# The last output column of a down projection in two halves of 256 features

## Chip, cores, metric

One core of one Trainium2 chip. The metric is the device time of one launch in microseconds (us), as the median of several runs. The profile is one execution, and its span (first to last instruction) is about 1.8 us shorter than the time of the profiled run. The record labels each run fast, slow (over 1.5% above the fastest of the same kernel, for a kernel on one core) or unknown.

## The reference, cut to what matters

```python
x = A_x                                    # [1, 2048, 512], bf16
xn = _layernorm(x, axis=-1)
return x + _A_ref(xn, A_w_r, A_w_i) + _B_ref(xn, B_w_gate, B_w_up, B_w_down)
# _A_ref: irfft2(rfft2(xn) * W), a spectral filter
# _B_ref: h = gelu(xn @ w_gate) * (xn @ w_up)   with 1792 hidden features
#         h @ w_down                            [2048, 1792] x [1792, 512]
```

## The kernel before

The kernel keeps everything in on-chip memory. A first stage loads and normalizes, a long middle stage makes the gate and up products (`h`, stored as tiles `hT`) with the spectral branch woven in, and a last stage makes the output. That last stage is what the change touches. The 2048 rows are 16 "columns" of 128 rows. For each column, 14 matmuls of the down projection and one of the inverse transform add up in one PSUM tile (the accumulator that the matmuls write) of 128x512 f32. VectorE then adds the residual `x` and SyncE's queue stores the column.

```python
    def down(c):
        sb, cl = c // 4, c % 4
        y_ps = ps.tile([P, D], F32, name="y_ps", tag="S", bufs=4)          # P = 128, D = 512
        for f in range(NFC):                                               # NFC = 14
            nc.tensor.matmul(y_ps[:], lhsT=hT[sb, f][:, cl * P:(cl + 1) * P], rhs=Wd_sb[:, f, :],
                             start=(f == 0), stop=False)
        nc.tensor.matmul(y_ps[:], lhsT=late["RI"][:, c, :], rhs=late["yt"][:, c, :], start=False, stop=True)
        y_sb = pw.tile([P, D], BF16, name="y_sb", bufs=3)
        nc.sync.dma_start(out=y_sb[:], in_=x_v[:, c, :])
        nc.vector.tensor_tensor(out=y_sb[:], in0=y_ps[:], in1=y_sb[:], op=ALU.add)
        nc.sync.dma_start(out=out_v[:, c, :], in_=y_sb[:])
    # ... (all earlier stages cut)
    for c in range(NC + 2):                                                # NC = 16
        if c < NC:
            idstep(c)        # last step of the spectral branch, writes yt
        if c >= 2:
            down(c - 2)
```

Of the kernel before, what the change touches and what calls it, by code (L numbers as in the profile page):

```python
# [10 lines left out]
P = 128  # L11
BF16 = mybir.dt.bfloat16
F32 = mybir.dt.float32
I32 = mybir.dt.int32
ALU = mybir.AluOpType
AF = mybir.ActivationFunctionType

S = 2048
D = 512
NC = 16  # L20
# [3 lines left out]
NFC = DF // P  # L24
# [99 lines left out]
def kernel(  # L124
# [11 lines left out]
    nc = tc.nc  # L136
# [6 lines left out]
    out_v = out.rearrange("b (p c) d -> p c (b d)", c=NC)  # L143
# [5 lines left out]
    ps = ctx.enter_context(tc.tile_pool(name="ps", bufs=2, space=bass.MemoryType.PSUM))  # L149
# [6 lines left out]
    Wd_sb = pc.tile([P, NFC, D], BF16, name="Wd_sb")  # L156
# [4 lines left out]
    late = {}  # L161
# [300 lines left out]
    hT = {}  # L462
# [22 lines left out]

    def down(c):
        sb, cl = c // 4, c % 4
        y_ps = ps.tile([P, D], F32, name="y_ps", tag="S", bufs=4)
        for f in range(NFC):
            nc.tensor.matmul(y_ps[:], lhsT=hT[sb, f][:, cl * P:(cl + 1) * P], rhs=Wd_sb[:, f, :],  # L490
                             start=(f == 0), stop=False)
        nc.tensor.matmul(y_ps[:], lhsT=late["RI"][:, c, :], rhs=late["yt"][:, c, :], start=False, stop=True)  # L492
        y_sb = pw.tile([P, D], BF16, name="y_sb", bufs=3)
        nc.sync.dma_start(out=y_sb[:], in_=x_v[:, c, :])
        nc.vector.tensor_tensor(out=y_sb[:], in0=y_ps[:], in1=y_sb[:], op=ALU.add)  # L495
        nc.sync.dma_start(out=out_v[:, c, :], in_=y_sb[:])


    first_columns()
# [45 lines left out]
    for c in range(NC + 2):  # L545
        if c < NC:
            idstep(c)
        if c >= 2:
            down(c - 2)
# [30 lines left out]
```

## Time and profile before

| | before |
|---|---|
| time, median of 3 runs | 185.38 us (185.33 to 185.46) |
| span of the profiled run | 183.77 us |
| TensorE busy | 172.2 us, 94% |
| last stage, first down matmul to end of span | 58.86 us |
| tail, start of the last matmul to end of span | 4.37 us |

The page's busy times (engine, busy us, share of the span, instructions) and its chain of the work that ended last:

```profile
PE 172.2 (94%) x1080; PEld 92.7 (50%) x1080; DVE 116.1 (63%) x273; ACT 97.8 (53%) x181; POOL 17.2 (9%) x52
...
PE 83%; DVE 4%; DMA 3%; POOL 3%; issue 3%; ACT 2%; ACTq 0%
```

PE is TensorE's matmuls, and they make 83% of the chain. Other engines' work is worth shortening where TensorE has nothing to do. That is so in the opening load stage (TensorE was busy for 13.6 of the first 20 us, the transfer engines for 94%), which this change leaves alone, and in the tail. This is the timeline of that tail, for TensorE and VectorE (start us, duration us, engine, line, operation, what it writes and reads, and in brackets what ended its idle time):

```profile
176.17 0.38 PE L492 MATMUL y_ps<-yt,RI_t 128*128 128x512 bf16 x1
...
176.38 3.18 PE L490 MATMUL y_ps<-Wd_sb,hT 128*128 128x512 bf16 x14
...
179.40 0.38 PE L492 MATMUL y_ps<-yt,RI_t 128*128 128x512 bf16 x1
179.82 0.69 DVE L495 TENSOR_TENSOR y_sb<-y_ps,y_sb 128x512 bf16<-128x512 f32 x1 [2.55 <-PE y_ps L492]
```

The first line is the last matmul of column 14, then come the 15 of column 15, one every 215.8 ns: (179.404 - 176.167) / 15. The sum waits for the last of them and takes 0.69 us. SyncE's view of the same tail (the issue of the last store, and what SyncE waited for after 180 us: total us, times, longest us):

```profile
180.54 0.33 SPq L496 DMA_DIRECT2D out_dram<-y_sb  x1
```

```profile
SPq L496 <- DVE y_sb L495: 2.9, 1, 2.9
SPq L575 <- DMA out_dram<-y_sb: 1.1, 1, 1.1
SPq L575 <- PEq L575: 1.1, 2, 0.9
```

So the order at the end is: last matmul, sum, store, landing of the store, closing waits (L575), end. A semaphore is a counter through which an engine learns that something is done; a store has landed when its semaphore has the full count. To see when the store moves its data, here are 40 slices of the window from 180.8 to 182.4 us, so 0.04 us each (share of the transfer engines in tenths, and rate):

```profile
DMA  0000000000000047899999973100000000000000
GB/s 0 0 0 0 0 0 0 0 0 0 0 0 0 0 154 256 307 358 410 358 384 358 333 231 103 26 0 0 0 0 0 0 0 0 0 0 0 0 0 0
```

Data flows in 12 slices, 0.48 us, of the 1.68 us from issue to landing. By the trace's packet records the first data packet starts 0.84 us after the issue, the last ends at 1.33 us, and the landing follows 0.35 us later.

### The profile page before, as it was taken

The numbers are of one execution on the slowest core, as the hardware profiler recorded it, in microseconds if no ns is written. First come the engines' busy times: TensorE is split into PE (matmuls) and PEld (weight loads), VectorE is DVE, ScalarE is ACT, GpSimd is POOL, SyncE is SP. The second block draws the span as 40 slices with busy tenths as digits, with TensorE's granted clock in tenths as the row PEclk, the third lists the DMA queues.
The fourth block names the chain that finished last, engine by engine and source line by source line (L and its number), as shares of the span: only waits on it lengthen the run. The fifth ranks groups of instructions, "written<-read, shape, count | busy, mean of one in ns | idle before, by whom it ended". The sixth has DMA issues, their size and how long they took to land.

```text
span 183.8 us, 3059 instructions
## 1 busy us (share of the span) xinstructions
PE 172.2 (94%) x1080; PEld 92.7 (50%) x1080; DVE 116.1 (63%) x273; ACT 97.8 (53%) x181; POOL 17.2 (9%) x52
## 2 busy tenths in 40 slices
PE   0699999899899999999999999999999999999991
PEld 0598974354445544554555554445445445445440
DVE  2679959972954599679778879835541541541611
ACT  2533568559888986988988875453211211211100
POOL 0000042177642000000000000000000000000000
PEclk9999999999999999999999999999999999999998
DMA  4999971404995001201392210100122221221210
GB/s 147 325 384 382 339 181 30 86 0 110 227 136 159 0 13 44 62 14 43 80 356 83 59 48 13 44 13 2 61 83 67 78 86 62 76 95 60 83 57 29
DMA packets 22062, 19.37 MB, mean 105 GB/s; under 512 B 8288, under 2 KB 20576, under 8 KB 22048
## 3 DMA queue, kind: packets, MB, share of 16 engines
q1 hardware_dynamic: 20816, 17.22, 33.2%
q0 software_dynamic: 416, 1.32, 3.1%
q10 hardware_dynamic: 816, 0.66, 1.1%
q8 instruction: 8, 0.13, 0.3%
q14 instruction: 6, 0.05, 0.1%
HBM read 13.41 MB, written 2.10 MB: 84 GB/s over the span
## 4 chain that ended last, share of the span: by engine, by line
PE 83%; DVE 4%; DMA 3%; POOL 3%; issue 3%; ACT 2%; ACTq 0%
PE y_ps L490 26%; PE g_ps L477 22%; PE u_ps L480 22%; DMA Wu_sb<-in_B_w_up_dram 3%; PE dp L346 2%; PE ep L358 2%; PE yp L445 2%; PE gp L430 2%; PE y_ps L492 2%; DVE hT L484 2%; PE bp L333 2%; ACT xn L273 1%; ACT ge L483 1%; DVE stats L257 1%; PE tp L306 1%
## 5 line engine op out<-in xcount | busy, mean ns | idle before, releaser
L477 PE MATMUL g_ps<-xnT,Wg_sb 128*128 128x512 bf16 (+2 forms) x276 | 62.3, 347 | 1.1 <-DMA xnT<-xn 0.5
L480 PE MATMUL u_ps<-xnT,Wu_sb 128*128 128x512 bf16 (+2 forms) x276 | 60.9, 344 | 0.1
L490 PE MATMUL y_ps<-Wd_sb,hT 128*128 128x512 bf16 x224 | 51.0, 379 | 0.0
L484 DVE TENSOR_TENSOR hT<-u_ps,ge 128x512 bf16<-128x512 f32 (+2 forms) x69 | 40.1, 583 | 15.0 <-PE u_ps L480 7.5
L483 ACT ACTIVATE ge<-g_ps 128x512 bf16<-128x512 f32 (+2 forms) x69 | 35.5, 520 | 21.2 <-PE g_ps L477 19.6
L480 PEld LDWEIGHTS <-Wu_sb 128*128 128x128 bf16 x276 | 26.6, 101 | 23.1 <-DMA Wu_sb<-in_B_w_up_dram 0.4
L477 PEld LDWEIGHTS <-Wg_sb 128*128 128x128 bf16 x276 | 25.8, 102 | 19.6 <-issue 2.0
L490 PEld LDWEIGHTS <-hT 128*128 128x128 bf16 x224 | 21.3, 98 | 23.1
L495 DVE TENSOR_TENSOR y_sb<-y_ps,y_sb 128x512 bf16<-128x512 f32 x16 | 11.1, 692 | 30.2 <-PE y_ps L492 30.2
L451 ACT CAST yf<-yp 128x512 bf16<-128x512 f32 x16 | 9.2, 587 | 37.3 <-PE yp L445 37.3
L361 ACT CAST E<-ep 64x512 bf16<-64x512 f32 x32 | 18.5, 579 | 3.7 <-PE ep L358 3.4
L339 ACT CAST Bs<-bp 128x512 bf16<-128x512 f32 x16 | 9.0, 586 | 3.4 <-PE bp L333 3.4
L339 ACT CAST ds<-dp 128x512 bf16<-128x512 f32 x16 | 9.2, 607 | 1.2 <-PE dp L346 1.2
L273 ACT ACTIVATE xn<-x_t,nb,rstd 128x512 bf16<-128x512 bf16 x12 | 9.4, 810 | 0.4 <-POOL nb L265 0.4
L339 ACT CAST Gs<-gp 128x512 bf16<-128x512 f32 x16 | 8.6, 591 | 1.4 <-PE gp L430 1.4
L257 DVE BATCH_NORM_STATS2 stats<-x_t 128x6 f32<-128x512 bf16 x14 | 9.2, 667 | 0.0
L383 DVE TENSOR_TENSOR X<-E 128x512 bf16<-128x512 bf16 x8 | 3.4, 426 | 8.6 <-ACT E L361 8.6
L306 PE MATMUL tp<-CT,xn 128*128 128x128 bf16 x16 | 2.0, 266 | 5.8 <-DVE xn L291 5.7
L445 PEld LDWEIGHTS <-Gs 128*128 128x128 bf16 x64 | 4.8, 98 | 3.3
L492 PE MATMUL y_ps<-yt,RI_t 128*128 128x512 bf16 x16 | 6.1, 379 | 0.0
L346 PE MATMUL dp<-CT,Bs 128*128 128x128 bf16 x64 | 6.0, 219 | 0.0
L333 PE MATMUL bp<-RF_t,xf 128*128 128x128 bf16 x64 | 5.4, 219 | 0.6 <-DVE xf L323 0.6
(67 smaller groups left out, 120.3 us busy)
## 6 DMA issues: line engine op xcount, KB each, us to landing
y_sb<-in_A_x_dram SPq DMA_DIRECT2D x16, 128.0 KB, 2.1
F<-F SPq DMA_DIRECT2D x32, 64.0 KB, 2.0
out_dram<-y_sb SPq DMA_DIRECT2D x16, 128.0 KB, 1.7
Wd_sb<-in_B_w_down_dram SPq DMA_DIRECT2D x1, 1792.0 KB, 8.8
x_t<-in_A_x_dram SPq DMA_DIRECT2D x3, 512.0 KB, 11.7
Wg_sb<-in_B_w_gate_dram SPq DMA_DIRECT2D x1, 768.0 KB, 9.0
Wu_sb<-in_B_w_up_dram SPq DMA_DIRECT2D x1, 768.0 KB, 10.6
Wg_sb<-in_B_w_gate_dram SPq DMA_DIRECT2D x2, 256.0 KB, 5.1
```

Of the source, the lines that this page charges most:

```text
L257: tc.keep_in_program_order(V.bn_stats(out=stats[:], in_=x_t[:, c, :]))
L273: nc.scalar.activation(out=xn[:, c, :], in_=x_t[:, c, :], func=AF.Identity, bias=nb[:, c:c + 1], scale=rstd[:, c:c + 1]))
L339: nc.scalar.copy(out=o, in_=i)
L346: nc.tensor.matmul(dp[:, q // 2, q % 2, :], lhsT=Bs[:, q, G].rearrange("p c r a -> p (c r a)"), rhs=FQ[q], start=(q == 0), stop=(q == 3), ...
L361: nc.scalar.copy(out=E[64 * h:64 * h + 64, r], in_=ep[64 * r:64 * r + 64])
L477: nc.tensor.matmul(gp[:], lhsT=Wg_sb[:, e, fc * P:(fc + 1) * P], rhs=rhs[:, e, :], start=(e == 0), stop=(e == NE - 1))
L480: nc.tensor.matmul(up[:], lhsT=Wu_sb[:, e, fc * P:(fc + 1) * P], rhs=rhs[:, e, :], start=(e == 0), stop=(e == NE - 1))
L483: nc.scalar.activation(out=ge[:], in_=gp[:], func=AF.Gelu_apprx_tanh)
L484: nc.vector.tensor_tensor(out=hT[sb, fc][:, o:o + w], in0=up[:], in1=ge[:], op=ALU.mult)
L490: nc.tensor.matmul(y_ps[:], lhsT=hT[sb, f][:, cl * P:(cl + 1) * P], rhs=Wd_sb[:, f, :], start=(f == 0), stop=False)
L492: nc.tensor.matmul(y_ps[:], lhsT=late["RI"][:, c, :], rhs=late["yt"][:, c, :], start=False, stop=True)
L495: nc.vector.tensor_tensor(out=y_sb[:], in0=y_ps[:], in1=y_sb[:], op=ALU.add)
```

## The change

The intent is to shorten the tail. In two halves, the first half's sum and store run under the second half's matmuls, and what is left exposed is a sum and a store of half the size.

```diff
     def down(c):
         sb, cl = c // 4, c % 4
-        y_ps = ps.tile([P, D], F32, name="y_ps", tag="S", bufs=4)
-        for f in range(NFC):
-            nc.tensor.matmul(y_ps[:], lhsT=hT[sb, f][:, cl * P:(cl + 1) * P], rhs=Wd_sb[:, f, :],
-                             start=(f == 0), stop=False)
-        nc.tensor.matmul(y_ps[:], lhsT=late["RI"][:, c, :], rhs=late["yt"][:, c, :], start=False, stop=True)
         y_sb = pw.tile([P, D], BF16, name="y_sb", bufs=3)
         nc.sync.dma_start(out=y_sb[:], in_=x_v[:, c, :])
-        nc.vector.tensor_tensor(out=y_sb[:], in0=y_ps[:], in1=y_sb[:], op=ALU.add)
-        nc.sync.dma_start(out=out_v[:, c, :], in_=y_sb[:])
+        w = D if c < NC - 1 else D // 2
+        for o in range(0, D, w):
+            y_ps = ps.tile([P, w], F32, name="y_ps", tag="S", bufs=4)
+            for f in range(NFC):
+                nc.tensor.matmul(y_ps[:], lhsT=hT[sb, f][:, cl * P:(cl + 1) * P], rhs=Wd_sb[:, f, o:o + w],
+                                 start=(f == 0), stop=False)
+            nc.tensor.matmul(y_ps[:], lhsT=late["RI"][:, c, :], rhs=late["yt"][:, c, o:o + w],
+                             start=False, stop=True)
+            nc.vector.tensor_tensor(out=y_sb[:, o:o + w], in0=y_ps[:], in1=y_sb[:, o:o + w], op=ALU.add)
+            nc.sync.dma_start(out=out_v[:, c, o:o + w], in_=y_sb[:, o:o + w])
```

## The prediction

> **What bounds the kernel now.** The page gives TensorE 94% busy of a 183.8 us span at a mean granted clock of 0.997, and the chain of work that ended last is 83% TensorE. The last stage is a pure TensorE stream: by the timeline, each output column of the down projection has 15 matmuls of 512 columns, 215.7 ns apart (3.24 us), with no idle time. Only the tail after the last matmul is exposed. The timeline of the last 8 us shows it: the first matmul of column 15 starts at 176.38, the last at 179.40; the residual sum (VectorE, 128x512) runs from 179.82 for 0.69 us; the store is issued at 180.54 and lands after about 1.7 us (median of the 16 stores); the span ends at 183.8. The DMA slices show data moving only from 181.3 to 181.85, about 0.4 us of work at 399 GB/s. So from the last matmul to the end there are about 4.2 us, of which 0.69 us (sum) and about 0.4 us (data) depend on the size of the last piece; the rest is latency and closing barriers.
>
> **What the change does.** It touches column 15 alone.
> - *Removed from the tail:* the last residual sum covers 256 instead of 512 features. The groups by form show the same kind of VectorE instruction (PSUM f32 + bf16 to bf16) at 683 ns for 128x512, 413 ns for 128x256 and 287 ns for 128x128. The Trainium skill, "VectorE: DVE Perf Modes", section on the TRN2 errata, gives (N+151)/0.96 ns, which is 691 for 512 (the trace: 691) and 424 for 256. I take 0.42: a gain of 0.27 us.
> - *Removed from the tail:* half the bytes of the last store, an estimate of 0.15 us (64 KB at about 390 GB/s is 0.17 us, against 0.33). The fixed part stays[...]. Rows become 512 bytes, so the gain may be less.
> - *Added on the critical path:* 30 matmuls of 256 columns instead of 15 of 512. The gate and up products already have 128x256 matmuls with a fresh weight load each, four in 0.437 us, 109.2 ns apart. So 3.276 us for 3.237: +0.04 us.
> - *Added off the path:* one more VectorE instruction and one more store (0.34 us of issue) under the second half's 1.6 us of matmuls. The first half's store should be issued near 178.5 and land near 180.2, before the second moves data. It uses another PSUM buffer, so no new wait.
> - *Moved:* the load of the residual is written ahead of the matmuls. It was already issued long before it is needed (172.35 for column 15), so nothing follows, unless the instruction order of other columns shifts.
>
> **Sum.** +0.04 - 0.27 - 0.15 = -0.38 us: 185.38 to 185.0 us, range 184.75 to 185.25. Faster by over 2%: 0.005; within 2%: 0.99; slower: 0.005.
>
> **What would show it.** TensorE starts column 15 at the same time; its last matmul starts near 179.55; the last VectorE sum is 0.42 us and starts near 179.86; the last store is issued near 180.3 and lands in about 1.55 us; the span shrinks to about 183.4. Right in sign but off in size: look at the store's landing and the matmul spacing.
>
> **What would make it wrong.** The second sum waiting for the first half's store to land (shared tile y_sb): then slower by about 0.4 us. Weight loads not hiding under 256-column matmuls here: up to +0.3 us. A store whose time to landing does not shrink with its bytes: gain only 0.23. A different instruction order in earlier columns: either way by a few tenths.

## The result, and the profile after

The first four runs had a median of 185.39 us (185.09 to 185.59) against 185.42 of four runs before. The ratio was 0.9984, with a 95% interval of 0.9961 to 1.0007. Ratios here are the mean time of one kernel's fast runs over that of the other's of the same rounds, so not quite the ratio of the medians. The means of all four runs against all four give 0.9997, so this first ratio is soft. Six more runs, in the experiments below, gave 185.18 us against 185.48, a ratio of 0.9978 (0.9963 to 0.9994). The second interval is wholly below 1.

The timeline of the tail after (columns as before):

```profile
176.49 0.38 PE L496 MATMUL y_ps<-yt,RI_t 128*128 128x512 bf16 x1
...
176.71 1.69 PE L494 MATMUL y_ps<-Wd_sb,hT 128*128 128x256 bf16 x14
...
178.23 0.27 PE L496 MATMUL y_ps<-yt,RI_t 128*128 128x256 bf16 x1
...
178.34 1.69 PE L494 MATMUL y_ps<-Wd_sb,hT 128*128 128x256 bf16 x14
178.54 0.42 DVE L498 TENSOR_TENSOR y_sb<-y_ps,y_sb 128x256 bf16<-128x256 f32 x1 [0.95 <-PE y_ps L496]
...
179.87 0.27 PE L496 MATMUL y_ps<-yt,RI_t 128*128 128x256 bf16 x1
180.18 0.42 DVE L498 TENSOR_TENSOR y_sb<-y_ps,y_sb 128x256 bf16<-128x256 f32 x1 [1.21 <-PE y_ps L496]
```

The first half's sum, at 178.54, lies wholly under the second half's matmuls. So does the issue of its store, as SyncE's line from 178 us on shows (two issues, the first at 179.00):

```profile
179.00 1.97 SPq L499 DMA_DIRECT2D out_dram<-y_sb  x2
```

The second sum took 0.42 us and waited for TensorE alone. SyncE's last issue and its waits after 180 us, and the rate in the same window of 180.8 to 182.4 us:

```profile
180.63 0.33 SPq L499 DMA_DIRECT2D out_dram<-y_sb  x1
```

```profile
SPq L499 <- DVE y_sb L498: 1.2, 1, 1.2
SPq L578 <- PEq L578: 1.1, 2, 0.9
SPq L578 <- DMA out_dram<-y_sb: 1.0, 1, 1.0
```

```profile
DMA  0000000000000000148999620000000000000000
GB/s 0 0 0 0 0 0 0 0 0 0 0 0 0 0 0 0 64 154 256 333 320 257 167 77 13 0 0 0 0 0 0 0 0 0 0 0 0 0 0 0
```

Half the bytes took 9 slices (0.36 us) instead of 12. The engines are as busy (9 tenths at the peak) at a lower rate: 333 GB/s against 410. The packet records say the same: a packet of 512 bytes took 26.8 ns in the mean and one of 1024 bytes 45.8. So rows of 512 bytes cost the engines more per byte here than rows of 1024.

**Absolute times mislead here.** The profiled run after came to column 15 at 176.49, 0.32 us later than the one before, though nothing that the change touches had run yet. The two traces show the same instructions in the same order on VectorE, ScalarE, GpSimd and SyncE up to column 15 (some matmul records are missing, so TensorE's can't be compared one by one). So the two spans (183.77 and 183.71) look almost equal while the tail is clearly shorter. The remedy is to anchor both traces at an event ahead of the change. From the start of column 14's last matmul, in ns, read from the trace's records:

| ns from the anchor to | before | after | difference |
|---|---|---|---|
| start of the last sum | 3654 | 3691 | +37 |
| end of the last sum | 4345 | 4114 | -231 |
| issue of the last store | 4373 | 4143 | -230 |
| landing of the last store | 6050 | 5723 | -327 |
| end of the span | 7607 | 7219 | -388 |

Term by term: +37 for the matmuls, -268 for the sum, -97 for the landing, and -61 between landing and end (the last 1 ns is at the issue). The last was in nobody's calculation, and -97 is less than the -150 predicted for the store. Both are followed up below.

### The profile page after: what moved, and what is told of

It reads as the page before. It is cut to its first block, busy times and chain, and to the rows that moved or that the text cites. A ratio compares the mean times of both kernels' runs of the same rounds, so it can differ in the third digit from the quotient of the medians.

```text
span 183.7 us, 3076 instructions
## 1 busy us (share of the span) xinstructions
PE 171.3 (93%) x1078; PEld 94.2 (51%) x1095; DVE 116.3 (63%) x274; ACT 97.9 (53%) x181; POOL 17.5 (10%) x52
## 4 chain that ended last, share of the span: by engine, by line
PE 78%; DVE 7%; ACT 5%; issue 4%; POOL 3%; DMA 2%; ACTq 0%
PE y_ps L494 26%; PE u_ps L480 21%; PE g_ps L477 19%; DVE hT L484 2%; PE y_ps L496 2%; PE yp L445 2%; PE dp L346 2%; PE ep L358 2%; PE gp L430 2%; DMA x_t<-in_A_x_dram 2%; ACT xn L273 2%; PE bp L333 1%; ACT Bs L339 1%; ACT E L361 1%; PE tp L306 1%
## 5 line engine op out<-in xcount | busy, mean ns | idle before, releaser
L477 PE MATMUL g_ps<-xnT,Wg_sb 128*128 128x512 bf16 (+2 forms) x266 | 61.3, 346 | 1.6 <-DMA xnT<-xn 0.8
L494 PE MATMUL y_ps<-Wd_sb,hT 128*128 128x512 bf16 (+1 forms) x233 | 50.7, 366 | 0.2
L494 PEld LDWEIGHTS <-hT 128*128 128x128 bf16 x238 | 22.7, 98 | 22.0
L498 DVE TENSOR_TENSOR y_sb<-y_ps,y_sb 128x512 bf16<-128x512 f32 (+1 forms) x17 | 11.2, 660 | 29.8 <-PE y_ps L496 29.8
L496 PE MATMUL y_ps<-yt,RI_t 128*128 128x512 bf16 (+1 forms) x17 | 6.2, 366 | 0.1
```

Source lines behind the costliest of these rows:

```text
L477: nc.tensor.matmul(gp[:], lhsT=Wg_sb[:, e, fc * P:(fc + 1) * P], rhs=rhs[:, e, :], start=(e == 0), stop=(e == NE - 1))
L498: nc.vector.tensor_tensor(out=y_sb[:, o:o + w], in0=y_ps[:], in1=y_sb[:, o:o + w], op=ALU.add)
```

## The experiments

The theory: the change acts on the tail alone, through four terms (matmuls, sum, landing, closing), and the gain exists because the first half hides under the second half's matmuls. The rivals: the difference is scatter of the opening load stage; it comes from the moved residual load; or small pieces are good wherever they stand.

The kernels ran with five rounds each (five or six runs), but for the first result (four runs) and the last two of the table, which had one look each. The record names another chip for each of the three groups of timed runs and for the last two, so times are compared only within a group. To compare profiles, I use the last stage's length, from the first down matmul to the end of the span. It includes every column. The control `move_only` agrees with the profile of the kernel before within 4 ns. The diffs are against the changed kernel, except where said.

| kernel | last stage, us | against before | median of time, us | ratio (95% interval) |
|---|---|---|---|---|
| before | 58.857 | | 185.38 | |
| move_only | 58.853 | -0.004 | 185.60 | 1.0004 (0.9989 to 1.0018) |
| after, first profile | 58.469 | -0.388 | 185.39 | 0.9984 (0.9961 to 1.0007) |
| after_again | 58.472 | -0.385 | 185.18 | 0.9978 (0.9963 to 0.9994) |
| matmul_halves_only | 58.902 | +0.045 | 185.62 | 1.0018 (0.9992 to 1.0045) |
| halves_one_store | 58.625 | -0.232 | 185.58 | 1.0001 (0.9985 to 1.0017) |
| sum_halves_only | 58.920 | +0.063 | 185.66 | 1.0015 (0.9994 to 1.0036) |
| split_384_128 | 58.246 | -0.611 | 184.82 | 0.9969 (0.9957 to 0.9982) |
| split_448_64 | 58.587 | -0.270 | 185.18 | 1.0004 (0.9981 to 1.0027) |
| all_columns_halves | 59.432 | +0.575 | 186.10 | 1.0048 (1.0031 to 1.0066) |
| before_four_more_loads | 58.614 | -0.243 | 185.20 | 0.9979 (0.9952 to 1.0006) |
| split_384_128_three_more_loads | 58.025 | -0.832 | 184.60 | 0.9954 (0.9923 to 0.9986) |
| before_one_more_load | 58.830 | -0.027 | 187.43, single run | |
| after_seven_more_loads | 58.476 | -0.381 | 187.10, single run | |

The kernel before had medians of 185.48, 185.37 and 185.40 us in the three groups of timed runs. In the group of the last two kernels its one run took 187.44 us; they came to the first down matmul 2 us later (126.8 us). I use only the last stage of these two, and their times not at all.

**The control first.** `move_only` keeps only the new line order of the change.

```diff
-        w = D if c < NC - 1 else D // 2
+        w = D if c < NC - 0 else D // 2    # true for every column: none is halved
```

> Only the line order of the change (the residual's load written ahead of the matmuls), no halves: the instructions of every engine stand in the same order as before. Theory: ratio 1 within 0.0005; it also shows the scatter of such a comparison. Rival (the moved load matters): a gain or loss of 0.2 us or more.

Its instructions stand in the same order as before (in the trace on VectorE, ScalarE, GpSimd and SyncE; some of TensorE's records are missing), and its last stage differs by 4 ns. Its profiled run took 186.17 us of time, though, because it came to the first down matmul at 125.51 us. Over the 12 profiles of the timed kernels that moment lies between 124.65 and 125.51 us. So the scatter of what comes ahead of it is about 0.9 us, and the last stage repeats within a few ns. The moved load does nothing. An effect of 0.2 us has to be read from the anchored trace, and the time can only confirm it roughly.

**The changed kernel again.**

> The changed kernel itself, more rounds. Theory (only the tail after the last matmul moves): from the start of column 14's last matmul to the end of the span 7.22 us against 7.61 us before, so 0.3 to 0.45 us less in time, ratio 0.9976 to 0.9984. Rival (nothing but scatter of the opening load stage, where the one profile of after stood 0.32 us later at column 15 than before): ratio within 0.0005 of 1.

The tail came out at 7.22 us a second time, and the time fell by 0.3 us by the medians. The rival of pure scatter falls, by the repeated tail above all: the interval of the ratio ends at 0.9994, just below 1.

**The matmuls alone.** Halves for TensorE, into one 512-wide tile, with one sum and one store (the diff is shortened).

```diff
+        y_ps = ps.tile([P, D], F32, name="y_ps", tag="S", bufs=4)
         for o in range(0, D, w):
-            y_ps = ps.tile([P, w], F32, ...)
             # 15 matmuls into y_ps[:, o:o + w], with skip_group_check=True (cut)
-            nc.vector.tensor_tensor(... o:o + w ...); nc.sync.dma_start(... o:o + w ...)
+        nc.vector.tensor_tensor(out=y_sb[:], in0=y_ps[:], in1=y_sb[:], op=ALU.add)
+        nc.sync.dma_start(out=out_v[:, c, :], in_=y_sb[:])
```

> The last column's 15 matmuls of 512 become 30 of 256 into one 512-wide tile, with one sum and one store as before: the cost of the change alone. Theory: +0.04 us (30 x 109.2 ns against 15 x 215.7 ns), the distance from column 14's last matmul to the sum's start 3.69 us against 3.65; ratio about 1.0002, not to be told from 1 by the time. Rival (fresh weight loads cost more here): over +0.15 us.

The timeline of TensorE in this kernel's last column:

```profile
176.02 0.38 PE L496 MATMUL y_ps<-yt,RI_t 128*128 128x512 bf16 x1
176.23 1.69 PE L494 MATMUL y_ps<-Wd_sb,hT 128*128 128x256 bf16 x14
177.76 0.27 PE L496 MATMUL y_ps<-yt,RI_t 128*128 128x256 bf16 x1
177.87 1.69 PE L494 MATMUL y_ps<-Wd_sb,hT 128*128 128x256 bf16 x14
179.40 0.27 PE L496 MATMUL y_ps<-yt,RI_t 128*128 128x256 bf16 x1
```

The second half starts 0.11 us after the first half's last matmul, with no gap: 15 matmuls in 1.638 us, 109.2 ns each, with a fresh weight load for every one. The sum starts 3.692 us after the anchor, 38 ns later than before. The cost of the change is those 38 ns; the stage grew by 45.

**Everything but the split store.**

```diff
-        w = D if c < NC - 1 else D // 2
-        for o in range(0, D, w):
+        ends = ((0, D),) if c < NC - 1 else ((0, 256), (256, 256))
+        for o, w in ends:
             # matmuls as in the changed kernel (cut)
             nc.vector.tensor_tensor(out=y_sb[:, o:o + w], in0=y_ps[:], in1=y_sb[:, o:o + w], op=ALU.add)
-            nc.sync.dma_start(out=out_v[:, c, o:o + w], in_=y_sb[:, o:o + w])
+        nc.sync.dma_start(out=out_v[:, c, :], in_=y_sb[:])
```

> Matmuls and sums in halves, one 128 KB store after the second sum: the change without its split store. Theory: the store is issued at the same 4.14 us after column 14's last matmul as in the changed kernel, but takes 1.68 us to land instead of 1.58, so the end comes 0.10 us later than there: 0.23 us less than before. Rival (the gain is all the smaller store): no gain against before.

The store went out 4.144 us after the anchor, as in the changed kernel, and took 1.674 us to land, as before. The stage gained 0.232 us. The time didn't show it (1.0001, with an interval that still holds 0.9987), which is the scatter again. The end came 0.156 us later than in the changed kernel, not the expected 0.10: the landing makes 0.094 of it, and the closing, from landing to end, was 1.557 us instead of 1.496, which I had not expected. So the closing term goes with the split store, not with the matmuls or the sum.

**Small pieces without anything to hide them.** One 512-wide accumulation, then two sums and two stores (the diff is shortened).

```diff
         # 15 matmuls of 512 columns into one y_ps, as before
+        for o in range(0, D, w):
+            nc.vector.tensor_tensor(out=y_sb[:, o:o + w], in0=y_ps[:, o:o + w], in1=y_sb[:, o:o + w], op=ALU.add)
+            nc.sync.dma_start(out=out_v[:, c, o:o + w], in_=y_sb[:, o:o + w])
```

> 15 matmuls of 512 as before, then two sums of 256 and two stores of 64 KB one after the other. Theory (the gain comes from hiding the first half's sum and store under the second half's matmuls): the second sum ends 0.75 to 0.8 us after the first starts, later than the single sum's 0.69; the last store lands 0.10 us sooner; together -0.1 to +0.05 us against before, no clear gain. Rival (smaller pieces are what counts): as fast as the changed kernel, -0.3 us.

VectorE's last column and SyncE's last issues in this kernel:

```profile
179.69 0.76 DVE L497 TENSOR_TENSOR y_sb<-y_ps,y_sb 128x256 bf16<-128x256 f32 x2 [2.55 <-PE y_ps L495]
```

```profile
180.15 0.81 SPq L498 DMA_DIRECT2D out_dram<-y_sb  x2
```

The two sums end 0.76 us after the first began, against 0.69 for the single one, and the two issues in one queue start 0.424 us apart (180.149 and 180.573). The second sum had ended at 180.451, so its store also stood behind the first one's issue. It also took 1.638 us to land, not about 1.58 as expected. So the landing came 0.120 us later than before, and the closing was 0.057 us shorter, as in the changed kernel. Result: 0.063 us longer, just above the range I had given. Smaller pieces gain nothing by themselves; the overlap does.

**Every column in halves.**

```diff
-        w = D if c < NC - 1 else D // 2
-        for o in range(0, D, w):
+        ends = ((0, 256), (256, 256))
+        for o, w in ends:
```

> Every one of the 16 columns in halves. Theory: 16 x 0.039 = 0.62 us more of matmuls, and the tail's gain once: +0.2 to +0.3 us against before. The residual sum's VectorE time grows but stays hidden. Rival (each halved column gains): faster than the changed kernel.

This was a miss: +0.575 us in the last stage instead of +0.2 to +0.3. Each halved column costs 37 to 38 ns, about 0.6 us for all, as expected. The rest is a new wait that I had not thought of, at the first column:

```profile
124.76 1.91 PE L494 MATMUL y_ps<-Wd_sb,hT 128*128 128x256 bf16 x16
126.89 0.27 PE L496 MATMUL y_ps<-yt,RI_t 128*128 128x256 bf16 x1 [0.22 <-DVE yt L458]
127.00 1.47 PE L494 MATMUL y_ps<-Wd_sb,hT 128*128 128x256 bf16 x12
```

The first half of column 0 reaches its matmul with `yt` after about 1.5 us of work instead of 3, and `yt` isn't ready. The starts 126.394 and 126.890 of neighbouring matmuls are 496 ns apart instead of 109, so 0.39 us are lost. The terms add up: +0.60 of matmuls, +0.39 of waiting, -0.27 of sum and -0.15 of landing (1.532 us instead of 1.677) make 0.57; the closing was as before, 1.558 us. A split also brings forward the moment at which its inputs are needed. At column 15 `yt` had long been ready.

**An uneven split, 384 and 128.**

```diff
-        w = D if c < NC - 1 else D // 2
-        for o in range(0, D, w):
+        ends = ((0, D),) if c < NC - 1 else ((0, 384), (384, 128))
+        for o, w in ends:
```

> The last column in 384 and 128 features. Theory: the last sum takes 0.29 us (gate stage, 128x128), 0.13 less than in the changed kernel; the last matmul ends at about the same time; the last store (32 KB, rows of 256 bytes) lands in 1.45 to 1.55 us. Together 0.13 to 0.25 us less than the changed kernel, 0.5 to 0.65 less than before. Rival (short rows make the store slower): the store takes over 1.58 us and the gain shrinks to that of the sum or less.

The timeline of the tail:

```profile
178.53 0.33 PE L496 MATMUL y_ps<-yt,RI_t 128*128 128x384 bf16 x1
...
178.70 0.95 PE L494 MATMUL y_ps<-Wd_sb,hT 128*128 128x128 bf16 x14
178.90 0.56 DVE L498 TENSOR_TENSOR y_sb<-y_ps,y_sb 128x384 bf16<-128x384 f32 x1 [1.75 <-PE y_ps L496]
...
179.48 0.22 PE L496 MATMUL y_ps<-yt,RI_t 128*128 128x128 bf16 x1
179.74 0.29 DVE L498 TENSOR_TENSOR y_sb<-y_ps,y_sb 128x128 bf16<-128x128 f32 x1 [0.28 <-PE y_ps L496]
```

The last sum starts 3.693 us after the anchor, as in the changed kernel, and takes 0.29 us. The first sum (0.56 us) just fits under the 15 small matmuls. The last store, 32 KB, landed in 1.490 us. The gain against before is 0.611 us in the stage, and the time agrees: 184.82 against 185.37 us. Rows of 256 bytes did not make the store slower than 1.58 us.

**A more uneven split, 448 and 64** (the same edit with those numbers).

> The last column in 448 and 64 features. Theory: the last sum takes about 0.22 us (151 + 64 cycles at the rate that fits 692 and 424 ns); 15 matmuls of 64 columns need more than their share, at 50 to 55 ns each, so +0.4 us of matmuls; the store of 16 KB lands in 1.45 us. The first store (448 wide) lands before the last one. Together about the same as the changed kernel: the matmuls take back what the sum gives.

VectorE's last column and SyncE's last issues:

```profile
179.21 0.75 DVE L498 TENSOR_TENSOR y_sb<-y_ps,y_sb 128x448 bf16<-128x448 f32 x2 [2.15 <-PE y_ps L496]
```

```profile
179.86 0.81 SPq L499 DMA_DIRECT2D out_dram<-y_sb  x2
```

The stage was longer than the changed kernel's by 0.118 us, near the expected "about the same", but for another reason than I gave. The 64-column matmuls cost no more than their share: 14 steps in 0.408 us, 29.1 ns each, fresh weight load included. What came out was a queue. The first sum (0.62 us) ends after the last matmul, so the second sum runs right behind it and ends at 179.965, and its store waits until 180.289 behind the first store's issue. The store of 16 KB took 1.510 us to land, not the expected 1.45, and longer than the 32 KB above. The larger first piece no longer hides.

**Where the 61 ns of closing come from.** The trace's records show SyncE's last eight waits for transfers. This is my listing of them: the landing of the last store, the time at which each wait was through, and the end, in us.

```
                        landed   wait 1  wait 2  wait 3  wait 4  wait 5  wait 6  wait 7  wait 8    end
before                 182.217  180.918 180.987 181.053 182.233 182.295 182.354 182.416 182.475  183.774
after                  182.212  181.009 181.078 181.145 181.209 182.228 182.287 182.349 182.408  183.708
before_four_more_loads 181.943  180.653 180.723 180.795 180.859 180.921 180.980 181.042 181.959  183.259
```

Each wait is for one of eight semaphores that the program's transfers use in turn (it also names a second semaphore, but none of those held it up here). Before, the last store had the fourth; four more waits follow its landing, about 61 ns each. The changed kernel has one more transfer, so its last store has the fifth and three waits follow. To test this without any halves, I gave the kernel before four more transfers in mid-stage, far from the tail (the diff is against the kernel before).

```diff
-        nc.sync.dma_start(out=y_sb[:], in_=x_v[:, c, :])
+        n = D // 2 if c in (4, 5, 6, 7) else D
+        for o in range(0, D, n):
+            nc.sync.dma_start(out=y_sb[:, o:o + n], in_=x_v[:, c, o:o + n])
```

> The kernel before, with the residual loads of columns 4 to 7 in two halves each: four more transfers in mid-stage, nothing else. Theory: the closing waits of SyncE go through eight transfer semaphores in a fixed order, 61 ns apart; the transfers take the eight in turn; the last store's was the fourth and becomes the eighth, so landing to end shrinks from 1.557 to about 1.31 us, 0.24 us less span with no half anywhere. Rival (the 0.06 us that the changed kernel's closing gained comes from the smaller store): landing to end stays 1.557.

The last store's wait became the eighth, and landing to end fell from 1.557 to 1.316 us. The stage gained 0.243 us, nearly as much as the halved sum gives, by nothing but the place of a semaphore. The median of the time fell by 0.2 us, though the interval of the ratio still holds 1. The closing term is shown, and it has nothing to do with the store's size.

**Why the second half store landed later than the first.** In the changed kernel the first 64 KB store landed in 1.527 us and the last in 1.580 (1.530 and 1.582 in the second profile), though their last data packets ended at nearly the same time after the issue, 1.177 and 1.171 us by the first profile. So the difference arises after the data, 0.350 us to landing for the first and 0.409 for the last. The first has the fourth semaphore, the last the fifth. Two single looks move semaphores with the same edit: in `before_one_more_load` for column 4, in `after_seven_more_loads`, applied to the changed kernel, for columns 4 to 10.

> The kernel before with the residual load of column 4 in two halves: one more transfer, so that the last store (still 128 KB) has the fifth semaphore, as in the changed kernel. Theory (the fifth semaphore shows a landing about 0.05 us later, whatever the size, and saves one closing wait): landing 1.72 to 1.73 us instead of 1.677, landing to end 1.496 instead of 1.557; the last stage 0.01 us shorter than before. Rival (the later landing of the changed kernel's last half has to do with half stores): landing 1.677, the last stage 0.06 us shorter.

> The changed kernel with seven residual loads (columns 4 to 10) in halves: the last store comes back to the fourth semaphore, which it has in the kernel before. Theory: it lands in 1.53 us instead of 1.58, as the first half's store does; landing to end is 1.557 instead of 1.496; last stage 0.37 to 0.38 us shorter than before. Rival (the second of two half stores is slower by its place): landing 1.58, last stage 0.33 us shorter than before.

| kernel, size of last store | its semaphore | issue to landing | landing to end | last stage against before |
|---|---|---|---|---|
| before, 128 KB | fourth | 1.677 | 1.557 | |
| before_one_more_load, 128 KB | fifth | 1.717 | 1.491 | -0.027 |
| after_seven_more_loads, 64 KB | fourth | 1.528 | 1.552 | -0.381 |
| after, 64 KB | fifth | 1.580 | 1.496 | -0.388 |

On the same semaphore, half the store lands 0.149 us sooner (1.677 to 1.528). The fifth one shows a landing 0.04 to 0.05 us later at either size, and saves about 0.06 us of closing. So the extra transfer's shift of semaphores is worth only about 0.01 to 0.03 us in all, and the rival, that the place of the half store matters, falls. The other stores agree: of the 128 KB stores in the kept traces whose data flowed alone, ten on the fourth semaphore landed in 1.672 to 1.687 us and five on the fifth in 1.717 to 1.758. Why the fifth semaphore shows a later landing no run tells.

**Both together.** The 384 and 128 split with three residual loads (columns 4 to 6) in halves, which gives its last store the eighth wait.

> The 384 and 128 split, with three residual loads (columns 4 to 6) in halves, so that the last store has the eighth semaphore: landing to end 1.31 instead of 1.496 us; 0.18 us less than the 384 and 128 split, 0.75 to 0.8 less than before (ratio about 0.9957). Rival: no more than the split alone, 0.9969.

Landing to end was 1.318 us, the last stage 0.832 us shorter than before (0.221 shorter than the plain 384 and 128 split), and the time 184.60 us against 185.40. The gain over the plain split is 0.04 us more than the expected 0.18, because the landing shortened as well: 1.447 us on the eighth semaphore, 1.490 on the fifth. This is the best version tried. It is still a gain of under half a percent.

## Why the prediction was right or wrong

The predicted time was 185.0 us with a range of 184.75 to 185.25. The first four runs had a median of 185.39, above that range, and their ratio put the kernel at 185.38 x 0.9984 = 185.08, but the ratio's interval reaches from 184.66 to 185.51. The six later runs had a median of 185.18. The predicted difference of -0.38 us is what the anchored trace shows (-0.388 and -0.385). Point by point:

- *The tail is what can be gained:* right. Nothing ahead of column 15 changed; the last stage of the control agreed within 4 ns.
- *+0.04 us of matmuls:* right, 37 to 38 ns, and isolated by `matmul_halves_only`.
- *-0.27 us of sum:* right, 691 to 423 ns. The Trainium skill, "VectorE: DVE Perf Modes", section on the TRN2 errata, gives (N+151)/0.96 ns for an f32 addition of two tensors. Estimates from that formula agree with the traces for 512, 256, 384 (557 by the formula, 556 measured) and 128 (291 and 291). For 64 it gives 224 and 211 were measured, but that sum started before the one ahead of it had ended.
- *-0.15 us of store:* right in size, 1.677 to 1.528 us on the same semaphore (1.532 in the timed kernel with all columns in halves). In the changed kernel it doesn't appear as such: the landing is only 0.097 us shorter, because the last store now has the fifth semaphore, which adds 0.05.
- *"The rest is latency and closing barriers", taken as fixed:* wrong. One more transfer moved the last store's semaphore from the fourth to the fifth closing wait, which took away 0.061 us and added those 0.05 to the landing. The two nearly cancel, so the total of the prediction held by luck. With another number of transfers they need not: four more were worth 0.243 us.
- *TensorE starts column 15 at the same time:* wrong for the pair of profiles, 0.32 us later. It was scatter of what comes ahead, up to 0.9 us over 12 profiles, which the prediction's range of +-0.25 us hardly allowed for.
- *The feared waits:* the second sum did not wait for the first store, and the weight loads hid. The order of instructions in earlier columns stayed the same.

What stays open: why a store on the fifth semaphore shows its landing 0.04 to 0.05 us later, and what makes the scatter ahead of the last stage.

## What to carry to other kernels

When one engine bounds a kernel, look at what it leaves behind after its last instruction. Split the last piece so that only a small remainder of the other engines' work is exposed, unevenly, and no further than the larger piece still hides under the smaller piece's matmuls (of the splits tried, 384 and 128 was best). Split only there: halving every column cost 0.6 us of matmuls and made a new wait at the front. And to judge an effect that is smaller than the scatter between runs, anchor both traces at an event ahead of the change, and take apart each stretch, the closing one too; a total that agrees can hide two terms that were left out.

## What the Trainium skill lacked or had wrong

- "TensorE: Matmul & The Clock Gate", section "Back-to-back issue gap", gives about 131 ns for a sustained matmul of 512 columns and 81 ns for 128, each with its weight load. (An earlier part of the same page gives 215.7 and 55.6 ns for back-to-back matmuls, so the page contradicts itself.) Here such streams ran at 215.8 ns for 512 columns and 55.8 ns for 128 (14 small matmuls of the 128-wide piece between their neighbours take 0.944 us less the first one's 162.5 ns, so 55.8 ns each). The page's formula for the isolated matmul, N/2.4 + 2.5 ns, fits the stream: also for 256 (109.2 measured), 384 (162.5) and 64 (29.1).
- "VectorE: DVE Perf Modes", the TRN2 errata: the formula is stated for f32 at 512 and 2048 columns. It also holds here for f32 from PSUM plus bf16 to bf16 at 128 to 512 columns, for sums that stand alone. At 64 it gives 224 ns and 211 were measured, but there the sum started 82 ns before the one ahead of it had ended; in `sum_halves_only` a 256-column sum in that position took 415 ns instead of 424. So no run tells whether the formula fails at 64.
- "DMA: Bandwidth & Descriptors", on the anatomy of a DMA, fits 2.0 us + bytes / 436 GB/s for the GpSimd path, most of the fixed part being the write receipt. It gives no such fit for SyncE's queue, on which 128 KB landed in 1.677 us here and 64 KB in 1.528. The slope agrees with the page's (64 KB / 436 GB/s gives an estimate of 0.150 us). The fixed part that this leaves is 1.38 us, and it doesn't lie mostly after the data: 0.84 us pass before the first data packet, and 0.35 us from the end of the last one to the landing.
- No page that I read tells that the closing waits for transfers come in a fixed order, one semaphore after the other, 61 ns each, so that the place of the last store's semaphore was worth 0.24 us here.
